# A long convolution with a soft mixture of experts: the order of VectorE's work at the odd part, and the filter's rotation on other engines

## The chip, the cores and the metric

The kernel runs on one core of a Trainium2 chip. The metric is the device time of one execution in microseconds (us); three executions of the kernel before took 959.56, 951.45 and 959.16 us, median 959.16. A core has five engines that run in parallel and wait for each other through semaphores: TensorE (PE in the profile, its weight loads PEld), VectorE (DVE), ScalarE (ACT), GpSimd (POOL), and SyncE (SP), which issues nearly all transfers here. Each engine takes its own instructions strictly in program order, so an instruction that waits holds up everything behind it on its engine. Transfers are done by 16 DMA engines. All data is float32.

## The reference

A causal convolution of 8 sequences of 5696 steps and 128 channels with a filter as long as the sequence, done by FFT, is followed by a mixture of experts with 32 soft slots.

```python
def _attn_ref(x, h):                       # x (8, 5696, 128), h (5696, 128)
    L = 2 * S
    Xf = np.fft.rfft(x, n=L, axis=1)
    Hf = np.fft.rfft(h, n=L, axis=0)
    y = np.fft.irfft(Xf * Hf[None], n=L, axis=1)[:, :S, :]
    return y

def _moe_ref(x, phi, w1, w2):              # x (45568, 128), phi (128, 32)
    logits = x @ phi
    d = softmax of logits over the tokens  # per slot
    slot_input = d.T @ x
    ...                                    # 8 experts on 4 slots each: relu(. @ w1) @ w2
    c = softmax of logits over the slots   # per token
    return c @ slot_out
```

The kernel computes the transform as two stages of matrix products (90 x 64 points). Stage A does the first stage on the inputs, stage B1 the second, the product with the filter's spectrum and stage B2 the first inverse stage; C1 does the last inverse stage, and C2 to C6 are the logits, the two softmaxes and the sums over tokens. Between A and B1, and between B2 and C1, the data goes through DRAM to change its layout (tensors `f` and `z`).

## The kernel before

The front loop goes through steps `t`. "Batch" 0 is the filter `h` itself; batches 1 to 8 are the sequences. In one step run stage A for one chunk of a batch, stage B for one or two units of the batch before it, and one half of the C stages of a pair of chunks of an earlier batch. A batch has 8 steps and 12 units; steps with one and with two units alternate.

Stage A folds the input on GpSimd (even and odd part), multiplies on TensorE, and copies out on ScalarE:

```python
    def fold(c, comp):
        ...
        nc.gpsimd.tensor_tensor(out=y_[:, :, :], in0=t_[:, 0, :, :], in1=t_[:, 1, ::-1, :],
                                op=AL.subtract if comp else AL.add)             # L201

    def stage_a(c, comp):
        ...
        for G in range(2):
            p = bank()
            nc.tensor.matmul(p[:, :], s1[:, tab[G], :], ...)                    # L212
            nc.scalar.activation(st[:, :, G, :], ..., AF.Copy)                  # L214
        # two transfers of st to f
```

Stage B1 is 16 matmuls into the PSUM tile `bt`. For a sequence, VectorE makes four instructions of them. For the filter (`g == 0`), each quarter of the unit is rotated by a phase of its own: ScalarE multiplies by the cosine, VectorE adds the sine's part, and `Hr`, `Hi` are kept for the whole kernel.

```python
    def stage_b1(u):
        ...
        tag = "bz" if g == 0 and w % 2 else "bt"
        bt = bps.tile([P, 2, 2, 2 * D], F32, name="bt", tag=tag)
        ...                                                                     # L250: 16 matmuls
        if g == 0:
            for o, (i, n) in enumerate(us):
                r = slice(0, n * HP)
                for a in range(2):
                    pv = bt[r, a, o, :].rearrange("p (c d) -> p c d", c=2)
                    tag = ("pr", "pi", "yf", "yf")[2 * o + a]
                    pr = bpool.tile([P, 2, D], F32, name="ph", tag=tag, ...)
                    nc.scalar.activation(pr[r, :, :], pv, AF.Copy,
                                         scale=turn[r, 0, i, a:a + 1])          # L261
                    nc.vector.scalar_tensor_tensor(                             # L262
                        out=Hr[r, w, a, o, :], in0=pv[:, 1, :], scalar=turn[r, 1, i, a:a + 1],
                        in1=pr[r, 0, :], op0=AL.mult, op1=AL.add)
                    nc.vector.scalar_tensor_tensor(                             # L265
                        out=Hi[r, w, a, o, :], in0=pv[:, 0, :], scalar=turn[r, 1, i, a:a + 1],
                        in1=pr[r, 1, :], op0=AL.mult, op1=AL.subtract, reverse1=True)
            return
        ...
        for p_, H_ in ((pr, Hr), (pi, Hi)):
            nc.vector.tensor_tensor(out=p_[r, 0:k, :, :], in0=pv, in1=..., op=AL.mult)   # L279
        y_ = bpool.tile([P, 4, 2, D], F32, name="yf", tag="yf", bufs=2)
        for c, op_ in ((0, AL.subtract), (1, AL.add)):
            nc.vector.tensor_tensor(out=y_[r, 0:k, c, :], in0=pr[...], in1=pi[...], op=op_)  # L284
```

Stage B2 (L299) multiplies `yf` into the PSUM tile `bz`, ScalarE copies it out (L304), and it is stored to `z`. A call `slot_b(n)` does B1 of the next unit and B2 of the one before it.

C1 makes an even and an odd part (L354). Its last piece is a function `after`, which the loop calls later. VectorE folds the odd part, and GpSimd makes four sums of it, which C2's transposes (L382) read in the next step:

```python
    def stage_c1(T, between):
        b_, a_ = product(0, 1, 1), product(0, 0, 0)
        nc.scalar.activation(part(0, 0), b_, AF.Copy)
        fold_out(a_, part(0, 0), part(1, 0))        # VectorE, two: L359, L360
        between()                                   # C4
        b_, a_ = product(1, 1, 0), product(1, 2, 1)
        nc.scalar.activation(om[:, :, :], b_, AF.Copy)                          # L367

        def after():
            fold_out(a_, om[:, :, :], op[:, :, :])  # VectorE, two: L359 writes op, L360 writes om
            for v, o_, eng in ((1, op, nc.gpsimd), (0, om, nc.vector if tail else nc.gpsimd)):
                for part_, sign in ((part(v, 1), AL.subtract), (part(v, 0), AL.add)):
                    eng.tensor_tensor(out=part_, in0=part(v, 0), in1=o_[:, :, :], op=sign)   # L373
        ...
        return after
```

The loop's order within a step, the parts that are not touched cut:

```python
    for t in range(last_front + 1):
        if t < NA:
            stage_a(t, 0)
            fold(t + 1, 0)
        if pair(3) is not None:
            dispatch(pair(3))
        if t < last_front:
            slot_b(1)
        ...
        if T is not None:
            after = stage_c1(T, rows)
        ...
        if pair(1) is not None:
            stage_c2(pair(1))
        if pair(5) is not None:
            stage_c6(pair(5))
        slot_b(2)
        ...                       # loads are issued
        if after:
            after()
        if U is not None:
            stage_c5(U)
        if t < NA:
            stage_a(t, 1)
            fold(t + 1, 1)
        if pair(1) is not None:
            stage_c3(pair(1))
        slot_b(3)
        ...                       # column_max, softmax
```

C1 and `after` come in the steps that have one unit, and that unit sits in `slot_b(2)`; the other steps have C2, C3 and two units, in slots 1 and 3.

Of the kernel before, what the change touches and what calls it, by code (L numbers as in the profile page):

```python
# [10 lines left out]
F32 = mybir.dt.float32  # L11
AF = mybir.ActivationFunctionType
AL = mybir.AluOpType
# [9 lines left out]
def transform_tables(S, N1, N2, CH, X0, F0, F1):  # L23

    N, R1, HALF, P = N1 * N2, S // N2, N2 // 2, 2 * N2
    k1 = np.arange(N1)
    alpha = np.pi * (k1 + 0.5) / N1
    m1 = np.arange(R1) - (N1 - 1) / 2
    a1 = np.outer(m1, alpha)  # L40
    s1 = np.stack([np.cos(a1), -np.sin(a1), -np.cos(a1)], 1)
    a0 = np.outer(alpha, np.arange(N1 // 2) + 0.5)
    i1 = np.stack([np.cos(a0), -np.sin(a0), -np.cos(a0)], 1)
    NP = N1 // 2
    part = s1
# [17 lines left out]
    tn = np.zeros((2, N2, 2, NU, 2))  # L63
    for a in range(2):
        wq[a] = w[a * NP:(a + 1) * NP].transpose(1, 0, 2)
        for q in range(NP):
            vq[q % 2, :, q // 2, a] = w[a * NP + q][back].T
            tn[q % 2, :, 0, q // 2, a] = np.cos(turn[a * NP + q]) / N
            tn[q % 2, :, 1, q // 2, a] = np.sin(turn[a * NP + q]) / N
# [5 lines left out]
def kernel(  # L75
# [24 lines left out]
    nc = tc.nc  # L100
    P = 128
    B, S, D = x.shape
# [4 lines left out]
    N1, N2 = 90, 64  # L107
    R1, HALF, NP = S // N2, N2 // 2, N1 // 2
# [7 lines left out]
    HP = P // 2  # L116
# [44 lines left out]
    s1 = apool.tile([P, 3, P], F32, name="s1", tag="s1", bufs=1)  # L161
    wt = fconst.tile([P, NP, HP], F32, name="wt")
    vt = fconst.tile([P, NU, 2, HP], F32, name="vt")
    turn = fconst.tile([P, 2, NU, 2], F32, name="turn")
    Hr = fconst.tile([P, NW, 2, 2, D], F32, name="Hr")
    Hi = fconst.tile([P, NW, 2, 2, D], F32, name="Hi")

# [73 lines left out]
    def stage_b1(u):  # L241
        g, w, us = parts(u)
        t_ = gs.pop(u)
# [4 lines that stand above are left out]
                r = slice(a * HP, (a + 1) * HP)  # L248
                for q in range(n):
                    nc.tensor.matmul(bt[q * HP:(q + 1) * HP, a, o, :], wt[r, 2 * i + q, :],  # L250
                                     t_[r, 2 * o + q, :, :].rearrange("p c d -> p (c d)"),
                                     start=True, stop=True)
        if g == 0:
            for o, (i, n) in enumerate(us):
                r = slice(0, n * HP)
                for a in range(2):
                    pv = bt[r, a, o, :].rearrange("p (c d) -> p c d", c=2)
                    tag = ("pr", "pi", "yf", "yf")[2 * o + a]
                    pr = bpool.tile([P, 2, D], F32, name="ph", tag=tag,
                                    bufs=2 if tag == "yf" else None)  # L260
                    nc.scalar.activation(pr[r, :, :], pv, AF.Copy, scale=turn[r, 0, i, a:a + 1])  # L261
                    nc.vector.scalar_tensor_tensor(  # L262
                        out=Hr[r, w, a, o, :], in0=pv[:, 1, :], scalar=turn[r, 1, i, a:a + 1],
                        in1=pr[r, 0, :], op0=AL.mult, op1=AL.add)
                    nc.vector.scalar_tensor_tensor(  # L265
                        out=Hi[r, w, a, o, :], in0=pv[:, 0, :], scalar=turn[r, 1, i, a:a + 1],
                        in1=pr[r, 1, :], op0=AL.mult, op1=AL.subtract, reverse1=True)
# [8 lines left out]
        pr, pi = [bpool.tile([P, 4, 2, D], F32, name=f"p{c}", tag=f"p{c}") for c in "ri"]  # L276
        for p_, H_ in ((pr, Hr), (pi, Hi)):
            h_ = H_[r, w, :, 0:m, :].rearrange("p a o d -> p (a o) d") if m == 2 else H_[r, w, :, 0, :]
            nc.vector.tensor_tensor(out=p_[r, 0:k, :, :], in0=pv,  # L279
                                    in1=h_.unsqueeze(2).broadcast_to([r.stop, k, 2, D]),  # L280
                                    op=AL.mult)
        y_ = bpool.tile([P, 4, 2, D], F32, name="yf", tag="yf", bufs=2)
        for c, op_ in ((0, AL.subtract), (1, AL.add)):
            nc.vector.tensor_tensor(out=y_[r, 0:k, c, :], in0=pr[r, 0:k, c, :],  # L284
                                    in1=pi[r, 0:k, 1 - c, :], op=op_)
        prods[u] = y_
# [275 lines left out]
    nc.scalar.dma_start(out=turn[:, :, :], in_=t_turn)  # L562
    nc.scalar.dma_start(out=i1[:, :, :], in_=t_i1)
    for comp in range(2):
        fold(0, comp)
# [2 lines left out]
    for t in range(last_front + 1):  # L568
        us = list(units(t))

        def pair(lag):
            T, half = divmod(t - LAG_C - lag, 2)
            return T if half == 0 and 0 <= T < NT else None
# [10 lines left out]
        def slot_b(place=None):  # L584
            if place is not None and place not in turns:
                return
            fresh = bool(us)
            if fresh:
                u = us.pop(0)
                prefetch(u + AHEAD)  # L590
                stage_b1(u)
                wait_b2.append(u)
            if len(wait_b2) > fresh:
                stage_b2(wait_b2.pop(0))
# [276 lines left out]
```

## Time and profile before

| what | value |
|---|---|
| median of three executions | 959.16 us |
| span of the profiled execution | 953.8 us |
| mean granted TensorE clock | 0.94 |
| data moved | 272.44 MB, mean 286 GB/s |
| filter's units in stage B1 | 55 to 119 us |
| C1 in the front loop | from 200 us |
| stage A's last matmul | 705 us |
| front loop's last unit in B1 | 792 us |

How to read the lines: a group or timeline line names the source line, the engine, the operation, and output<-inputs by tile names; x16 is a count; in square brackets stands the idle time of the engine before the instruction and what ended it. A wait line has the total in us, the number of times and the longest. A busy TensorE is not a TensorE at its peak, since the ends of its matmuls are modelled. Four groups that the change touches, from the page (busy us in total, mean ns of one, idle us before and what ended it):

```profile
L201 POOL TENSOR_TENSOR x<-xc 128x512 f32<-128x512 f32 x144 | 196.2, 1370 | 179.7 <-PE bank L212 134.1
...
L284 DVE TENSOR_TENSOR yf<-pr,pi 128x512 f32<-128x512 f32 x192 | 184.8, 1003 | 3.3
L279 DVE TENSOR_TENSOR pr<-bt,Hr 128x1024 f32<-128x1024 f32 x96 | 113.1, 1178 | 88.9 <-PE bt L250 87.3
...
L373 POOL TENSOR_TENSOR y<-y,op 128x512 f32<-128x512 f32 x64 | 77.9, 1217 | 106.6 <-DVE op L359 104.1
```

### The profile page before, as it was taken

To read this page: it belongs to the slowest core of one execution; us is meant where nothing else is said; L and a number is where in the kernel's file an instruction comes from. 1 tells how busy PE (TensorE), PEld (TensorE's weight loads), DVE (VectorE), ACT (ScalarE), POOL (GpSimd) and SP (SyncE) were. 2 spreads that over 40 slices of the span, in tenths; PEclk is the share of its full clock that TensorE was granted. 3 is DMA by queue.
4 is the path that set the end of the run, shared out by engine and by line. 5 is a ranking of instruction groups with operands and counts; after the bars stand their busy time and mean duration, and the time that the engine had idled before them with its cause. 6 is when DMAs were issued, how large, how long until landed. Compare 5 with 4: busy or idle time off the path is not lost.

```text
span 953.8 us, 19381 instructions
## 1 busy us (share of the span) xinstructions
PE 830.5 (87%) x7220; PEld 423.3 (44%) x7220; DVE 688.8 (72%) x972; ACT 501.6 (53%) x934; POOL 429.0 (45%) x385
## 2 busy tenths in 40 slices
PE   6867697879999999999999999999998887777893
PEld 2322243334444444444444444444444443344783
DVE  3024488776987888899889888888888897583552
ACT  3535544444655565656555656555654444375442
POOL 4623333334565555555555555565542334372000
PEclk9979999998999999999999999999999898797865
DMA  9978899999899999998999899999979887862698
GB/s 289 262 236 228 229 308 316 312 332 291 279 284 298 311 296 305 320 311 258 309 304 319 273 319 329 328 288 312 303 255 303 267 292 197 259 226 92 236 405 344
DMA packets 156552, 272.44 MB, mean 286 GB/s; under 512 B 11766, under 2 KB 114422, under 8 KB 153317
## 3 DMA queue, kind: packets, MB, share of 16 engines
q1 hardware_dynamic: 155883, 270.85, 88.7%
q8 instruction: 58, 0.95, 0.4%
q10 hardware_dynamic: 576, 0.36, 0.2%
q14 instruction: 35, 0.29, 0.1%
HBM read 142.85 MB, written 128.21 MB: 284 GB/s over the span
## 4 chain that ended last, share of the span: by engine, by line
PE 42%; DMA 19%; DVE 16%; POOL 13%; issue 5%; ACT 3%; SPq 2%; DVEq 0%; ACTq 0%; POOLq 0%
PE bank L212 14%; PE bank L354 10%; POOL y L373 9%; PE bt L250 7%; DMA gt<-f 5%; DMA out_dram<-o 4%; DVE yf L284 4%; DVE pr L279 4%; DMA f<-fst 4%; DVE pi L279 3%; POOL x L201 3%; PE bz L299 3%; PE bank L391 2%; DMA zd<-z 2%; PE bank L420 2%
## 5 line engine op out<-in xcount | busy, mean ns | idle before, releaser
L212 PE MATMUL bank<-x,s 128*128 128x512 f32 x576 | 281.9, 625 | 23.8 <-POOL x L201 16.9
L201 POOL TENSOR_TENSOR x<-xc 128x512 f32<-128x512 f32 x144 | 196.2, 1370 | 179.7 <-PE bank L212 134.1
L214 ACT ACTIVATE fst<-bank 128x512 f32<-128x512 f32 x288 | 167.1, 597 | 95.0 <-PE bank L212 63.8
L304 ACT ACTIVATE zst<-bz 128x1024 f32<-128x1024 f32 x96 | 93.3, 972 | 183.5 <-PE bz L299 180.5
L284 DVE TENSOR_TENSOR yf<-pr,pi 128x512 f32<-128x512 f32 x192 | 184.8, 1003 | 3.3
L279 DVE TENSOR_TENSOR pr<-bt,Hr 128x1024 f32<-128x1024 f32 x96 | 113.1, 1178 | 88.9 <-PE bt L250 87.3
L212 PEld LDWEIGHTS bank<-x,s 128*128 128x128 f32 x576 | 104.2, 196 | 148.5 <-issue 96.1
L250 PE MATMUL bt<-gt,wt 64*64 64x256 f32 x1620 | 117.8, 397 | 30.9 <-DMA gt<-f 21.5
L373 POOL TENSOR_TENSOR y<-y,op 128x512 f32<-128x512 f32 x64 | 77.9, 1217 | 106.6 <-DVE op L359 104.1
L354 PE MATMUL bank<-zc,i 128*64 128x512 f32 x480 | 116.4, 606 | 2.2 <-DMA zc<-z 1.6
L279 DVE TENSOR_TENSOR pi<-bt,Hi 128x1024 f32<-128x1024 f32 x96 | 112.2, 1169 | 0.0
L299 PE MATMUL bz<-yf,vt 64*64 64x256 f32 x1440 | 102.3, 385 | 5.8 <-DVE yf L284 5.7
L250 PEld LDWEIGHTS bt<-gt,wt 64*64 64x64 f32 x1620 | 54.8, 135 | 109.7 <-issue 38.9
L382 PE MATMUL bank<-ident,y 109*128 109x109 f32 x512 | 66.1, 273 | 19.2 <-POOL y L373 18.4
L262 DVE SCALAR_TENSOR_TENSOR Hr<-bt,turn,ph 128x128 f32<-128x128 f32 (+1 forms) x46 | 16.1, 350 | 81.1 <-ACT ph L261 81.1
L299 PEld LDWEIGHTS bz<-yf,vt 64*64 64x64 f32 x1440 | 58.7, 136 | 31.6 <-issue 10.3
L382 PEld LDWEIGHTS bank<-ident,y 109*128 109x128 f32 x512 | 52.0, 147 | 38.7 <-POOL y L373 29.1
L373 POOL TENSOR_TENSOR y<-y,om 128x512 f32<-128x512 f32 x54 | 64.5, 1195 | 2.1
L384 ACT ACTIVATE yt<-bank 128x360 f32<-128x360 f32 x128 | 54.1, 474 | 15.5 <-PE bank L382 15.2
L354 PEld LDWEIGHTS bank<-zc,i 128*64 128x64 f32 x480 | 29.3, 136 | 63.7 <-issue 44.0
L428 POOL MEMSET dt<- 64x8 f32 x32 | 3.5, 108 | 116.9 <-issue 57.6
L824 PE MATMUL op<-so,cT 32*128 32x128 f32 x704 | 46.2, 368 | 4.3 <-ACT o L833 3.7
(96 smaller groups left out, 876.0 us busy)
## 6 DMA issues: line engine op xcount, KB each, us to landing
f<-fst SPq DMA_DIRECT2D x288, 180.0 KB
gt<-f SPq DMA_DIRECT2D x99, 512.0 KB
z<-zst SPq DMA_DIRECT2D x88, 512.0 KB
zc<-z SPq DMA_DIRECT2D x30, 1024.0 KB
xc<-in_x_dram SPq DMA_DIRECT2D x64, 320.0 KB
out_dram<-o SPq DMA_DIRECT2D x16, 1024.0 KB
zc<-z SPq DMA_DIRECT2D x30, 416.0 KB
out_dram<-o SPq DMA_DIRECT2D x8, 768.0 KB
```

The source lines that it names most:

```text
L201: nc.gpsimd.tensor_tensor(out=y_[:, :, :], in0=t_[:, 0, :, :], in1=t_[:, 1, ::-1, :], op=AL.subtract if comp else AL.add)
L212: nc.tensor.matmul(p[:, :], s1[:, tab[G], :], src[:, :, :].rearrange("p n d -> p (n d)"), start=True, stop=True)
L214: nc.scalar.activation(st[:, :, G, :], p[:, :].rearrange("p (n d) -> p n d", d=D), AF.Copy)
L250: nc.tensor.matmul(bt[q * HP:(q + 1) * HP, a, o, :], wt[r, 2 * i + q, :], t_[r, 2 * o + q, :, :].rearrange("p c d -> p (c d)"), start=True ...
L279: nc.vector.tensor_tensor(out=p_[r, 0:k, :, :], in0=pv, in1=h_.unsqueeze(2).broadcast_to([r.stop, k, 2, D]), op=AL.mult)
L284: nc.vector.tensor_tensor(out=y_[r, 0:k, c, :], in0=pr[r, 0:k, c, :], in1=pi[r, 0:k, 1 - c, :], op=op_)
L299: nc.tensor.matmul(bz[a * HP:(a + 1) * HP, q, o, :], vt[r, i, a, :], y_[r, a * m + o, :, :].rearrange("p c d -> p (c d)"), start=True, sto ...
L304: nc.scalar.activation(st[:, 0:m, 0:n, :].rearrange("p o q x -> p q o x"), bz[:, 0:n, 0:m, :], AF.Copy)
L354: nc.tensor.matmul(p[h_ * HP:(h_ + 1) * HP, :], i1[0:kr, tab, :], t_[0:kr, h_, o, :, q, :], start=True, stop=True)
L373: eng.tensor_tensor(out=part_, in0=part(v, 0), in1=o_[:, :, :], op=sign)
L382: nc.tensor.transpose(p[:, i * TR:(i + 1) * TR], ys[T][0:TR, k * CH + i, 0:D], ident[0:TR, 0:TR])
L384: nc.scalar.activation(yt[:, k * CH:(k + 1) * CH, :, :], of_tokens(p), AF.Copy)
```

## The change

It has two parts. First, `after` is called ahead of `slot_b(2)`, so that VectorE folds the odd part, and GpSimd begins its sums, before VectorE takes up the products and sums of that step's unit. Its instructions are the same; nothing changes on TensorE's own order. Second, the filter's rotation is done like the product of a sequence's unit: VectorE multiplies the whole unit in PSUM by the cosine and by the sine (two instructions of up to 1024 elements a partition), and GpSimd adds and subtracts them into `Hr` and `Hi` (two of up to 512). The four ScalarE copies and eight small VectorE instructions of a unit go. The table `turn` gets a layout that can be read as one operand, and the products use the tiles `pr`, `pi` and, for every second unit, the two `yf` buffers.

```diff
-    turn = fconst.tile([P, 2, NU, 2], F32, name="turn")
+    turn = fconst.tile([P, 2, NW, 2, 2], F32, name="turn")
...
-        if g == 0:
-            for o, (i, n) in enumerate(us):
-                r = slice(0, n * HP)
-                for a in range(2):
-                    pv = bt[r, a, o, :].rearrange("p (c d) -> p c d", c=2)
-                    tag = ("pr", "pi", "yf", "yf")[2 * o + a]
-                    pr = bpool.tile([P, 2, D], F32, name="ph", tag=tag,
-                                    bufs=2 if tag == "yf" else None)
-                    nc.scalar.activation(pr[r, :, :], pv, AF.Copy, scale=turn[r, 0, i, a:a + 1])
-                    nc.vector.scalar_tensor_tensor(
-                        out=Hr[r, w, a, o, :], in0=pv[:, 1, :], scalar=turn[r, 1, i, a:a + 1],
-                        in1=pr[r, 0, :], op0=AL.mult, op1=AL.add)
-                    nc.vector.scalar_tensor_tensor(
-                        out=Hi[r, w, a, o, :], in0=pv[:, 0, :], scalar=turn[r, 1, i, a:a + 1],
-                        in1=pr[r, 1, :], op0=AL.mult, op1=AL.subtract, reverse1=True)
-            return
...
+        tags = ("yf", "yf") if g == 0 and w % 2 else ("pr", "pi")
+        pr, pi = [bpool.tile([P, 4, 2, D], F32, name="p", tag=x, bufs=2 if x == "yf" else 1)
+                  for x in tags]
+        for p_, H_ in ((pr, turn[:, 0]), (pi, turn[:, 1])) if g == 0 else ((pr, Hr), (pi, Hi)):
...                               # h_: the operand, broadcast to the shape of pv
+            nc.vector.tensor_tensor(out=p_[r, 0:k, :, :], in0=pv, in1=h_, op=AL.mult)
+        if g == 0:
+            for c, op_, H_ in ((0, AL.add, Hr), (1, AL.subtract, Hi)):
+                h_ = H_[r, w, :, :, :].rearrange("p a o d -> p (a o) d") if m == 2 else H_[r, w, :, 0, :]
+                nc.gpsimd.tensor_tensor(out=h_, in0=pr[r, 0:k, c, :], in1=pi[r, 0:k, 1 - c, :],
+                                        op=op_)
+            return
...
         if pair(5) is not None:
             stage_c6(pair(5))
+        if after:
+            after()
         slot_b(2)
...
-        if after:
-            after()
         if U is not None:
             stage_c5(U)
```

Cut: the change of the table's layout on the host side, and the load of `turn`, which differs in its shape alone.

More of the change, by code (lines that the diff above doesn't have):

```diff
@@ L62, in transform_tables @@
     vq = np.zeros((2, N2, NU, 2, N2))
-    tn = np.zeros((2, N2, 2, NU, 2))
+    tn = np.zeros((2, N2, 2, (NU + 1) // 2, 2, 2))
     for a in range(2):
@@ L67, in transform_tables @@
             vq[q % 2, :, q // 2, a] = w[a * NP + q][back].T
-            tn[q % 2, :, 0, q // 2, a] = np.cos(turn[a * NP + q]) / N
-            tn[q % 2, :, 1, q // 2, a] = np.sin(turn[a * NP + q]) / N
+            tn[q % 2, :, 0, q // 4, a, q // 2 % 2] = np.cos(turn[a * NP + q]) / N
+            tn[q % 2, :, 1, q // 4, a, q // 2 % 2] = np.sin(turn[a * NP + q]) / N
     wq, vq, tn = [t.reshape(P, *t.shape[2:]) for t in (wq, vq, tn)]
@@ L275, in stage_b1 @@
         k = 2 * m
[L276 to L281, printed above, removed]
+        tags = ("yf", "yf") if g == 0 and w % 2 else ("pr", "pi")
+        pr, pi = [bpool.tile([P, 4, 2, D], F32, name="p", tag=x, bufs=2 if x == "yf" else 1)
+                  for x in tags]
+        for p_, H_ in ((pr, turn[:, 0]), (pi, turn[:, 1])) if g == 0 else ((pr, Hr), (pi, Hi)):
+            if g:
+                h_ = H_[r, w].rearrange("p a o d -> p (a o) d") if m == 2 else H_[r, w, :, 0]
+            else:
+                h_ = (H_[r, w].rearrange("p a o -> p (a o)") if m == 2 else H_[r, w, :, 0]).unsqueeze(2)
+                h_ = h_.broadcast_to([r.stop, k, D])
+            h_ = h_.unsqueeze(2).broadcast_to([r.stop, k, 2, D])
+            nc.vector.tensor_tensor(out=p_[r, 0:k, :, :], in0=pv, in1=h_, op=AL.mult)
[5 more added lines that the diff above has]
+            return
         y_ = bpool.tile([P, 4, 2, D], F32, name="yf", tag="yf", bufs=2)
@@ L561 @@
     nc.scalar.dma_start(out=phi[:, :], in_=moe_phi)
-    nc.scalar.dma_start(out=turn[:, :, :], in_=t_turn)
+    nc.scalar.dma_start(out=turn[:, :, :, :, :], in_=t_turn)
     nc.scalar.dma_start(out=i1[:, :, :], in_=t_i1)
```

## The prediction

> **What bounds the kernel now.** I read the page's busy shares, then a table of stretches, the table of waits, and the timeline of one two-step period.
>
> ```profile
> PE 830.5 (87%) x7220; PEld 423.3 (44%) x7220; DVE 688.8 (72%) x972; ACT 501.6 (53%) x934; POOL 429.0 (45%) x385
> ```
>
> ```profile
> 57.00:119.00 62.00, 45.58 (x240) 18.80 (x244) 28.02 (x92) 36.40 (x78) 20.31 (x16) 0.94 0.78 222
> 228.00:701.00 473.00, 457.51 (x3996) 224.63 (x3994) 406.74 (x527) 278.13 (x504) 267.95 (x230) 1.00 0.95 304
> 701.00:800.00 99.00, 80.44 (x856) 42.43 (x852) 84.06 (x120) 44.37 (x80) 34.79 (x35) 0.91 0.84 263
> ```
>
> The first line is the whole span. The three stretches give length, then busy us of PE, weight load, DVE, ACT and POOL, the clock, the DMA share and GB/s. From 57 to 119 us the filter's units run beside the first batch's forward stage: no engine is busy for more than 74% and the DMA share is only 0.78. From 228 to 701 TensorE is busy 97%, with the DMA engines at 0.95. From 701 on the forward stage has ended and VectorE leads with 85%. Between 119 and 200 us TensorE stops mainly for loads; nothing of the change touches a load.
>
> ```profile
> POOL y L373 <- DVE op L359: 104.1, 29, 7.6
> ...
> DVE Hr L262 <- ACT ph L261: 81.1, 46, 48.0
> ...
> ACT ph L261 <- DVE Hi L265: 24.9, 34, 0.7
> ...
> PE bank L382 <- POOL y L373: 18.4, 38, 1.1
> ...
> PE bank L212 <- POOL x L201: 16.9, 23, 8.7
> ```
>
> Waits over the whole span: total us, times, longest. The second and third are the filter's ping-pong: ScalarE copies a quarter of a unit, VectorE makes two results of it, and ScalarE waits for them before it copies the next. (48 of the 81.1 us is the wait for the first unit.) The other three are one chain: VectorE's fold of the odd part releases GpSimd's four sums, which release the transposes, and behind them GpSimd's fold of the next input releases the forward matmul.
>
> ```profile
> 411.03 1.22 DVE L279 TENSOR_TENSOR pr<-bt,Hr 128x1024 f32<-128x1024 f32 x1
> ...
> 413.42 1.29 DVE L284 TENSOR_TENSOR yf<-pr,pi 128x512 f32<-128x512 f32 x2
> ...
> 414.63 0.68 DVE L359 TENSOR_TENSOR op<-bank,om 128x512 f32<-128x512 f32 x1
> ...
> 415.39 2.44 POOL L373 TENSOR_TENSOR y<-y,op 128x512 f32<-128x512 f32 x2 [3.24 <-DVE op L359]
> ...
> 420.30 0.59 PE L382 MATMUL bank<-ident,y 109*128 109x109 f32 x4 [0.27 <-POOL y L373]
> ...
> 421.52 1.98 PE L212 MATMUL bank<-x,s 128*128 128x512 f32 x4 [0.26 <-POOL x L201]
> ```
>
> The timeline of one period (22.43 us from one moved unit's matmuls to the next): start, length, instruction, idle time before it. The odd part's inputs are ready at 410.1, where the copy to om ends, but VectorE first does a unit's two products and two yf sums, 411.03 to 414.6. So GpSimd idles 3.24 us, finishes its four sums late, and TensorE stops twice.
>
> **What the skill says.** The Trainium skill, "SBUF — State Buffer", section "Who interferes with whom": a VectorE instruction with two SBUF inputs contends with a GpSimd one that reads SBUF, and the second to issue is blocked; with one SBUF input it does not. The trace agrees: the yf sums (two SBUF inputs) take 0.65 us when GpSimd rests and up to 1.77 us, while the products from PSUM stay at 1.22 and the folds of op at 0.68 to 0.69. "GPSIMD Engine Reference", section "2.1 Instruction dispatch": about 2.5 cycles an element for two inputs; at its 1.2 GHz that is an estimate of 1.07 us for 512 elements, and the trace has 1.05 to 1.37. "ScalarE: Activation LUTs", section "What ACT_TABLE_LOAD costs": 186 ns plus 0.833 ns an element plus 93 ns for a pointer operand, an estimate of 492 ns for 256 elements; the trace has 478 for the copies that go.
>
> **The filter, part by part.** Removed: 46 ScalarE copies of 0.478 us (22 us) and 92 small VectorE results of 0.35 us (32 us), which the stretch 57 to 119 consists of. One link takes 1.21 us (copies start at 69.86 and 71.07), so 46 links are 55.7 us of the 62, the rest being the forward stage's own ScalarE copies in between. Added for each of 12 units: two VectorE products of the form that already takes 1.22 us (29 us in all; only 2.4 us of latency a unit) and two GpSimd sums of 512 elements at about 1.2 us (24 x 1.2 = 29 us). GpSimd's 20.3 us in this stretch become 49. TensorE's 45.6 us stay, and moving the same data (62 us x 222 GB/s = 13.8 MB) at the 300 GB/s of the later stages takes 46 us. So three things stand at 46 to 49 us, and GpSimd works in order: the fold of the next input waits behind a sum that waits for products. I take 55 us for the stretch: 7 us gained. It should stay gained, since transfers of the next stage only start earlier.
>
> **The odd part.** Nothing is added; in 27 steps two VectorE folds move ahead of four instructions. In the period shown op would start at 411.03, so GpSimd's sums start when its own row-maximum subtraction ends, at 412.2 instead of 415.4, and end about 417.2. TensorE reaches the transposes at 418.7: both stops vanish. They are 0.53 us of shown idle time; matmul starts, 0.53 us apart at the stop where 0.09 is usual, and as much at the forward matmul, make it about 0.8 us a period. Against it: the products start 1.35 us later, their yf sums at 414.8 fall on GpSimd's busy time and take up to 3 us instead of 1.29, so they end near 418.0, and the matmul of that unit, due at 417.71, waits 0.3. Half a microsecond or so remains: 21 periods x 0.5 = 10. The DMA share of 0.95 would have to become 0.975; I take off a fifth: 8 us. The first period (202 to 228) idles 2.7 us for the same reason, but comes out of the load-bound stage: 1.5. After 701, four periods idle about 2.5 us each for these sums, but there TensorE gets to the moved unit's matmul sooner, and would now wait for yf instead: 2.5 us for all four.
>
> Sum: 7 + 8 + 1.5 + 2.5 = 19; 959 - 19 = 940. The profiled execution took 955.5, so the median lies high in its spread and I put 939.
>
> **Rivals.** (a) GpSimd becomes the filter stage's bound. Its folds sit in one queue with the sums; if each sum waits for its products without overlap, a unit costs 2.4 + 2.4 us in series, the 4.8 of before, and the stage gains nothing and 12 us remain: about 947. For it speaks the in-order queue, against it the two sets of product buffers that alternate. (b) The DMA engines are the true bound from 228 on: the share of 0.95 at 304 GB/s is near the 1.02 at 337 GB/s of the stretch 140 to 160. Then the freed TensorE only waits for loads, or ScalarE for buffers of stores, and the steady stage gives 2 us instead of 8: 946. Against it: TensorE has no wait for a DMA between 228 and 701. (c) VectorE becomes the bound: 20.2 us of a 22.4 us period, plus what the lock adds. If the moved unit's sums cost 2 us more and nothing else gets cheaper, nothing is gained in the steady or the late stage: 951. Against it: the next unit's sums, 2.85 us today because GpSimd works beside them, would fall into a quieter time. (d) Everything goes as meant: the filter stage falls to 50 us, all 0.8 us a period are gained, the late stage gains 2 us a period: 12 + 17 + 2 + 8 = 39, 920.
>
> **Range and chances.** Rivals (a) to (c) would end at 946 to 951, two of them together near 953; (d) at 920. The three times of before spread over 8 us. Range 924 to 954. The 2% line is 940.0, on my estimate: faster by over 2% 0.50, within 2% 0.45. Slower by over 2% needs a blockage that I can't see, such as the filter's sums holding up the forward stage: 0.05.
>
> **What would show it.** The start of the first plain product on bt (119.8 us now) should be near 113. GpSimd's wait for op should fall from 104 us by about 60, the two TensorE waits on GpSimd from 35 us to under 8, and the wait of bz for yf should rise from 5.7 us to some 10. Periods between 228 and 701 should be 0.3 to 0.5 us shorter. The yf sums should show a like total (184.8 us), shifted between units. The prediction is wrong if the first product on bt stays after 117, if TensorE begins to wait for gt or zc between 228 and 701, or if VectorE is busy over 97% there.

## The result and the profile after

| kernel | median us | ratio to the kernel before, with 95% interval |
|---|---|---|
| before, beside it | 956.52 (951.45 to 959.56) | |
| changed | 928.75 (926.44 to 929.01) | 0.9709 [0.9657, 0.9762] |
| changed, measured again | 934.37 (925.43 to 935.86), before 957.83 | 0.9755 [0.9711, 0.9799] |

The change saves 27.8 us (956.52 - 928.75), and 23.5 us in the second measurement. The predicted time was 939, the range 924 to 954.

To see where the time went I cut both traces at the same events: the first plain product on `bt`, the first copy to `om` (the first C1), the second and the 23rd copy to `om`, and the last unit's B1. Each kernel was profiled twice; a cell has the two durations in us, and the last column compares the means.

| stage | before | changed | change of the mean | predicted |
|---|---|---|---|---|
| start to first plain product | 119.8, 118.9 | 108.1, 109.6 | -10.5 | -7 |
| to the first C1 (loads) | 82.3, 80.5 | 79.7, 80.4 | -1.3 | 0 |
| first period with C1 | 26.4, 26.4 | 20.5, 22.1 | -5.1 | -1.5 |
| the next 21 periods | 472.6, 472.5 | 460.6, 463.9 | -10.3 | -8 |
| late stage, to the last unit | 90.6, 90.6 | 90.6, 90.8 | +0.1 | -2.5 |
| the rest (no front loop) | 162.1, 162.9 | 167.1, 167.2 | +4.6 | 0 |

The page's busy line of the changed kernel (busy us, share of the span, instructions):

```profile
PE 820.8 (89%) x7220; PEld 423.8 (46%) x7220; DVE 681.4 (74%) x904; ACT 475.7 (51%) x888; POOL 456.3 (49%) x409
```

The 46 ScalarE copies are gone (934 instructions became 888), and GpSimd has 24 sums more (385 became 409). The table of waits over the whole span (total us, times, longest us):

```profile
DVE p L270 <- PE bt L250: 107.4, 37, 46.0
...
ACT fst L214 <- DMA f<-fst: 59.1, 32, 5.1
...
PE bz L294 <- DVE yf L279: 16.5, 13, 2.3
PE bank L212 <- POOL x L201: 13.0, 8, 8.2
...
POOL y L368 <- DVE op L354: 8.6, 4, 4.1
```

Both parts did their work: the ping-pong's two waits are gone, GpSimd's wait for `op` fell from 104.1 to 8.6 us, and TensorE's wait for the four sums, 18.4 us before, is no longer there. Two waits grew in their place: ScalarE's wait for a free store buffer (`fst`, 23.8 before) and TensorE's for `yf` (5.7 before). The table of stretches (length, busy us of PE, weight load, DVE, ACT, POOL with counts, clock, DMA share, GB/s), of the changed kernel:

```profile
57.00:106.00 49.00, 41.50 (x227) 16.17 (x225) 25.73 (x23) 18.90 (x32) 44.93 (x37) 0.99 0.88 266
187.80:208.40 20.60, 20.40 (x160) 9.21 (x156) 16.71 (x19) 11.88 (x21) 10.59 (x8) 1.00 1.02 332
...
228.00:701.00 473.00, 458.94 (x4135) 229.87 (x4135) 410.07 (x548) 274.48 (x514) 267.50 (x233) 1.00 0.97 310
```

In the filter's stage GpSimd has become the busiest engine (44.93 of 49 us), and the DMA share rose from 0.78 to 0.88. The second line is the first period with C1; it is used below. In the stretch from 228 to 701 us, in whose last 27 us stage A has ended here, the DMA share rose from 0.95 to 0.97. One period of the changed kernel, on its timeline (start, length, instruction, idle before):

```profile
383.68 0.68 DVE L354 TENSOR_TENSOR op<-bank,om 128x512 f32<-128x512 f32 x1
...
384.91 2.45 POOL L368 TENSOR_TENSOR y<-y,op 128x512 f32<-128x512 f32 x2
385.00 1.22 DVE L270 TENSOR_TENSOR p<-bt,Hr 128x1024 f32<-128x1024 f32 x1
...
387.32 2.77 POOL L368 TENSOR_TENSOR y<-y,om 128x512 f32<-128x512 f32 x2
...
387.38 3.26 DVE L279 TENSOR_TENSOR yf<-p 128x512 f32<-128x512 f32 x2
...
391.09 1.04 PE L294 MATMUL bz<-yf,vt 64*64 64x256 f32 x16
...
392.07 1.72 PE L377 MATMUL bank<-ident,y 109*128 109x109 f32 x16
```

GpSimd starts its sums without idling and ends them at 390.1, two microseconds before the transposes at 392.07: TensorE's stop is gone. The price stands in the `yf` line: the two sums took 1.29 us in the period shown of before and take 3.26 here, because they now lie beside GpSimd's four. They end at 390.64, still 0.45 us before the matmul that needs them.

### The profile page after: what moved, and what is told of

Same layout as the page of the kernel before. It is cut to its first block, busy times and chain, and to the rows that moved or that the text cites. A ratio compares the mean times of both kernels' runs of the same rounds, so it can differ in the third digit from the quotient of the medians.

```text
span 926.6 us, 19311 instructions
## 1 busy us (share of the span) xinstructions
PE 820.8 (89%) x7220; PEld 423.8 (46%) x7220; DVE 681.4 (74%) x904; ACT 475.7 (51%) x888; POOL 456.3 (49%) x409
## 4 chain that ended last, share of the span: by engine, by line
PE 52%; DMA 23%; DVE 11%; POOL 4%; SPq 4%; issue 3%; ACT 2%; DVEq 0%; ACTq 0%; POOLq 0%
PE bank L212 17%; DMA f<-fst 10%; PE bank L349 9%; PE bt L250 6%; PE bz L294 6%; PE bank L377 4%; DVE yf L279 4%; DVE p L270 4%; DMA out_dram<-o 4%; DMA zd<-z 3%; PE bank L462 2%; DMA zc<-z 2%; DMA gt<-f 2%; PE bank L415 1%; PE op L819 1%
## 5 line engine op out<-in xcount | busy, mean ns | idle before, releaser
L212 PE MATMUL bank<-x,s 128*128 128x512 f32 x576 | 275.5, 612 | 14.8 <-POOL x L201 13.0
L279 DVE TENSOR_TENSOR yf<-p 128x512 f32<-128x512 f32 x192 | 187.9, 1019 | 3.3
L212 PEld LDWEIGHTS bank<-x,s 128*128 128x128 f32 x576 | 101.8, 192 | 133.6 <-issue 89.0
L270 DVE TENSOR_TENSOR p<-bt,Hr 128x1024 f32<-128x1024 f32 x96 | 112.8, 1175 | 61.9 <-PE bt L250 58.0
L250 PE MATMUL bt<-gt,wt 64*64 64x256 f32 x1620 | 115.5, 392 | 19.1 <-DMA gt<-f 11.9
L294 PE MATMUL bz<-yf,vt 64*64 64x256 f32 x1440 | 102.2, 385 | 16.5 <-DVE yf L279 16.5
L270 DVE TENSOR_TENSOR p<-bt,Hi 128x1024 f32<-128x1024 f32 x96 | 112.2, 1169 | 0.0
L250 PEld LDWEIGHTS bt<-gt,wt 64*64 64x64 f32 x1620 | 54.6, 133 | 95.5 <-issue 22.6
L368 POOL TENSOR_TENSOR y<-y,op 128x512 f32<-128x512 f32 x64 | 77.4, 1210 | 11.2 <-DVE op L354 8.6
L270 DVE TENSOR_TENSOR p<-bt,turn 128x1024 f32<-128x1024 f32 (+1 forms) x24 | 27.2, 1174 | 68.3 <-PE bt L250 49.4
L368 POOL TENSOR_TENSOR y<-y,om 128x512 f32<-128x512 f32 x54 | 72.8, 1348 | 2.1
L377 PE MATMUL bank<-ident,y 109*128 109x109 f32 x512 | 60.7, 277 | 0.7 <-DVE y L368 0.7
L379 ACT ACTIVATE yt<-bank 128x360 f32<-128x360 f32 x128 | 50.9, 480 | 2.8 <-PE bank L377 2.7
```

The costliest lines, as they stand in the source:

```text
L212: nc.tensor.matmul(p[:, :], s1[:, tab[G], :], src[:, :, :].rearrange("p n d -> p (n d)"), start=True, stop=True)
L270: nc.vector.tensor_tensor(out=p_[r, 0:k, :, :], in0=pv, in1=h_, op=AL.mult)
L294: nc.tensor.matmul(bz[a * HP:(a + 1) * HP, q, o, :], vt[r, i, a, :], y_[r, a * m + o, :, :].rearrange("p c d -> p (c d)"), start=True, sto ...
L377: nc.tensor.transpose(p[:, i * TR:(i + 1) * TR], ys[T][0:TR, k * CH + i, 0:D], ident[0:TR, 0:TR])
```

## The experiments

Theory: the two parts act apart from each other; the filter's stage is shorter because the ping-pong is gone, and is now limited by transfers and by GpSimd together; the order frees TensorE in every period, but the transfers take a part of it back; in the late stage the order exchanges one wait for another. The rivals are named with each experiment. Two kernels that leave work out, and the kernel before where it is profiled again, were executed once and have no interval.

### Each part alone

The filter's part alone (in the changed kernel the call is moved back), and the order alone (in the kernel before the call is moved ahead):

```diff
# filter only, on the changed kernel
-        if after:                 # ahead of slot_b(2)
-            after()
...
+        if after:                 # after the loads
+            after()
# order only, on the kernel before: the same move the other way
```

> The filter's rotation as changed, the odd part's sums where they were before. If the two parts act in their own stages: the first plain product on bt near 108 us, the first copy to om near 188 to 190, the periods after it as before (22.4 to 22.8 us), GpSimd's wait for op near 100 us again; time 956.5 - 14 = about 942 us, ratio about 0.985. Rival, the gain of the filter stage is only kept because the later stages are quick enough to use it: the first copy to om back near 200 us, time about 953 us, ratio 0.997.

> The odd part's sums moved, the filter's rotation as before. If the parts act in their own stages: first plain product on bt near 120 us, first copy to om near 202, then a first period about 5 us shorter and 21 periods about 0.57 us shorter, and 0 to 5 us given back behind the front loop; time 956.5 - 14 to - 18 = 939 to 942 us, ratio 0.982 to 0.985, and the two gains add up to the change's 27.8. Rival, the first period's 5.8 us belong to the filter (data had been moved earlier): the first period stays at 26 us here, time about 945 us.

| kernel | median us | ratio, 95% interval | first plain product | first period | 21 periods | late | rest |
|---|---|---|---|---|---|---|---|
| filter only | 946.72 | 0.9913 [0.9887, 0.9939] | 107.3 | 26.6 | 472.4 | 90.6 | 165.5 |
| order only | 941.48 | 0.9861 [0.9800, 0.9922] | 116.6 | 22.7 | 462.9 | 91.6 | 165.8 |

The product of the two ratios is 0.9775, with an interval of some 0.0066 to each side (the root of the two half-widths, 0.0026 and 0.0061, squared and added). That meets both intervals of the changed kernel, so the parts add, as far as these measurements tell. The stages keep them apart too: only the filter's part shortens the first stage by 12 us (the 2 to 3 us of the order alone lie ahead of anything that it moves, and show how far traces differ there), only the order shortens the first period and the 21 that follow, and neither shortens the late stage.

### What limits the filter's stage now

The changed kernel's timeline in this stage, VectorE, GpSimd and TensorE:

```profile
68.55 2.36 DVE L270 TENSOR_TENSOR p<-bt,turn 128x1024 f32<-128x1024 f32 x2 [1.33 <-issue]
68.61 1.27 POOL L274 TENSOR_TENSOR Hi<-p 128x512 f32<-128x512 f32 x1
...
69.84 1.26 POOL L201 TENSOR_TENSOR x<-xc 128x512 f32<-128x512 f32 x1
...
71.16 1.55 PE L212 MATMUL bank<-x,s 128*128 128x512 f32 x3 [0.81 <-POOL x L201]
```

GpSimd works back to back, and TensorE's forward matmul waits 0.81 us for its fold. That reads as if GpSimd were the bound. Two kernels test it: one moves half of the filter's sums to VectorE, the other leaves out all loads of `x` (the filter `h` is still loaded, the sequences are computed from whatever lies in the buffers), which takes 23 of 272 MB away.

```diff
# half of the filter's sums on VectorE
-                nc.gpsimd.tensor_tensor(out=h_, in0=pr[r, 0:k, c, :], ...
+                (nc.vector if c else nc.gpsimd).tensor_tensor(out=h_, in0=pr[r, 0:k, c, :], ...
# no loads of x
-        for r in (slice(0, SPLIT), slice(SPLIT, R1)):
+        for r in (slice(0, SPLIT), slice(SPLIT, R1)) if g == 0 else ():
```

> The changed kernel with one of the filter's two sums on VectorE (0.65 us a unit there when GpSimd rests) instead of GpSimd. Theory, GpSimd is the bound of the filter's stage now (44.9 us busy of the 49 from 57 to 106): the stage loses up to 12 x 1.2 us of GpSimd's time, the first plain product on bt comes near 101 instead of 108 us, where TensorE's 41 us and the transfers stop it, and 3 to 7 us are kept at the end. Rival, the transfers are the bound (share 0.88 at 266 GB/s): the first plain product stays within 2 us of 108.

> The changed kernel without the loads of x (the filter's input h is still loaded; stage A works on what is left in its buffers, so the result is not the convolution). It takes away 23 MB of 272 and nothing else. Theory, the DMA engines are the bound that is left: the filter's stage gets shorter, the first plain product on bt comes near 102 instead of 108 to 110 us, the first copy to om near 175 instead of 188 to 190, the 21 steady periods come down from 461 to 464 to about 454 us, and ScalarE's wait for stores of f falls under 20 us. Rival, GpSimd's queue holds the filter's stage and TensorE the steady one: 107 us, and 460 us.

The stretch of this stage, of the kernel with the divided sums and then of the one without loads of `x` (its stage ends earlier, so its stretch is 44 us):

```profile
57.00:106.00 49.00, 41.00 (x227) 16.34 (x225) 34.09 (x35) 19.11 (x32) 39.28 (x28) 0.99 0.89 272
```

```profile
57.00:101.00 44.00, 36.95 (x218) 14.53 (x218) 23.89 (x21) 16.22 (x28) 40.14 (x33) 1.00 0.78 225
```

With 5.7 us taken off GpSimd (44.93 to 39.28) the first plain product came at 107.3 us; the nine traces that have the filter's part with its sums on GpSimd and all loads lie between 106.7 and 109.6, so this is no difference. The time was 928.46 us, ratio 0.9717 [0.9664, 0.9770], beside 0.9755 [0.9711, 0.9799] of the changed kernel measured with it: no difference that the intervals show. Without the loads of `x` the product came at 103.6 us (908.88 us in all, one execution). But there the filter's first unit began its matmuls at 49.7 us already, in the changed kernel at 53.5 and 54.8. From this start to the first plain product both kernels take 53.9 us, the changed one 54.6 and 54.8: neither edit shortens the stage itself by more than a microsecond. The chain of work that ended last shows what holds it, in the stretches above: the changed kernel, then with the divided sums, then without the loads of `x` (share of the stretch by engine and line; "issue" is time in which the engine waited for nothing that the profile shows):

```profile
by line: PE bank L212 31.3%; DMA xc<-in_x_dram 18.1%; POOL x L201 17.2%; POOL Hi L274 11.8%; issue 9.0%; SPq L218 3.7%; POOL Hr L274 3.1%; SPq L190 2.5%; ACT fst L214 2.5%; SPq L236 1.8%; PE bt L250 1.2%; POOLq L201 0.2%
```

```profile
by line: DMA gt<-f 35.6%; PE bank L212 23.4%; DMA xc<-in_x_dram 9.6%; DMA f<-fst 6.5%; issue 6.3%; POOL x L201 5.2%; PE bt L250 4.5%; SPq L218 3.8%; ACT fst L214 3.7%; SPq L236 1.2%; SPq L190 1.1%; POOL Hr L274 0.1%; POOLq L201 0.1%
```

```profile
by line: POOL x L201 23.3%; POOL Hi L274 22.8%; POOL Hr L274 20.8%; issue 18.7%; PE bank L212 14.3%; PE bt L250 1.3%; POOLq L201 0.0%
```

With GpSimd relieved, its part of the chain falls from 32% to 5% and the transfers' rises from 18% to 52%; without the loads of `x` no transfer is left in it, and GpSimd has 67%. (In the changed kernel's second trace GpSimd has 46% and the transfers 6%.) So the two stand at nearly the same height, and relieving one alone leaves the other. Both at once were not tried. Moving GpSimd's sums elsewhere by itself is not worth it here.

### What the order is worth in the steady stage, and who takes it back

The kernel without loads of `x` tells this too. TensorE's table of waits from 208.4 to 669 us, in the changed kernel:

```profile
PE bank L415 <- ACT fst L214: 5.3, 9, 1.5
PE bank L349 <- DMA zc<-z: 2.2, 3, 1.3
PE bt L250 <- DMA gt<-f: 1.3, 2, 1.0
PE bt L250 <- DVE yf L279: 0.2, 1, 0.2
```

Before, TensorE had no wait for `zc` and none or 0.4 us for `gt` in these periods, but 15.1 and 14.1 us for GpSimd (two traces). Now the waits for GpSimd are gone, and 8.8 of the 9.0 us that remain lead to transfers: to loads, or to ScalarE that could not free a PSUM bank because its store buffer was still being read. The stretch from 228 to 660 us, first the changed kernel and then the one without loads of `x`:

```profile
228.00:660.00 432.00, 422.68 (x3746) 211.33 (x3745) 373.21 (x496) 253.66 (x474) 251.85 (x218) 1.00 0.98 311
```

```profile
228.00:660.00 432.00, 431.23 (x3844) 212.39 (x3836) 387.02 (x503) 262.68 (x479) 254.50 (x220) 1.00 0.88 284
```

In the same 432 us the second did 98 matmuls more, with TensorE busy for all but 0.8 us and the DMA share at 0.88. Its 21 periods took 452.2 us. Measured from 472.5 that is 20.3 us, 0.97 a period; the changed kernel keeps 8.7 to 12.0 of it, and the transfers hold back 8 to 12 us. (The seven other traces with the new order and all work vary more, from 460.2 to 468.0 us; the mean of all nine, 463.8, keeps 8.7 us.) (The kernel before was not run without the loads of `x`; since it had next to no wait for a transfer in these periods, I take it that it would have gained little, and the split of the 20.3 us is an estimate.)

Is it the number of store buffers, or the transfers themselves? A fourth `fst` buffer tells:

```diff
-        st = apool.tile([P, CH, 2, D], F32, name="fst", tag="fst", bufs=3)
+        st = apool.tile([P, CH, 2, D], F32, name="fst", tag="fst", bufs=4)
```

> The changed kernel with four instead of three buffers for stage A's results. Theory, the DMA engines are what is left as the bound in the steady stage: ScalarE's wait for stores of f (59 us) falls, but TensorE then waits longer for loads of gt and zc, and the 21 steady periods stay within 2 us of 460. Rival, it is only the count of buffers: TensorE's 5.4 us of waits behind ScalarE's fst vanish, the steady stage becomes 455, and the time 5 us shorter.

TensorE's waits from 210 to 670 us in this kernel:

```profile
PE bank L349 <- DMA zc<-z: 3.9, 6, 1.3
PE bt L250 <- DMA gt<-f: 2.2, 5, 1.0
...
PE bank L349 <- ACT fst L214: 0.6, 1, 0.6
```

The wait behind `fst` is 0.6 us, where it was 5.3 (6.6 in the changed kernel's second trace). But TensorE's idle time in the 21 periods is 10.1 us, beside 9.3 and 13.0, with 6.1 of it behind `zc` and `gt`, and the periods took 460.2 us, beside 460.6 and 463.9. The buffer was the place where the shortage showed, not its cause. The kernel's time was 925.52 us, 0.9666 [0.9617, 0.9715], better than that of the changed kernel measured with it (0.9755 [0.9711, 0.9799]) with intervals that just touch. In its trace the gain lies in the rest, 160.3 us instead of 167, where no buffer of stage A is in use. What makes it stays open: on top of another edit (below, "the same, four fst") the fourth buffer gave nothing that the intervals show, and the 21 periods took 464.8 us there.

### The late stage: one wait for another

Stage A's last matmuls end 5 us after the 23rd copy to `om`. TensorE's table of waits in this stage, of the kernel before:

```profile
PE bank L382 <- POOL y L373: 8.8, 15, 0.7
PE bank L467 <- ACT d L446: 3.8, 4, 1.0
```

and of the changed kernel:

```profile
PE bz L294 <- DVE yf L279: 9.5, 5, 2.3
PE bank L462 <- ACT d L441: 3.8, 4, 1.0
```

The wait for GpSimd was exchanged for one of the same size for VectorE, and the stage stayed at 90.6 us. The timeline of the changed kernel shows its form:

```profile
688.33 2.45 POOL L368 TENSOR_TENSOR y<-y,op 128x512 f32<-128x512 f32 x2
...
690.73 2.77 POOL L368 TENSOR_TENSOR y<-y,om 128x512 f32<-128x512 f32 x2
690.80 3.25 DVE L279 TENSOR_TENSOR yf<-p 128x512 f32<-128x512 f32 x2
...
694.20 1.09 PE L294 MATMUL bz<-yf,vt 64*64 64x256 f32 x16 [2.03 <-DVE yf L279]
```

The Trainium skill, "SBUF — State Buffer", section "Who interferes with whom", names the cause: these VectorE sums have two SBUF inputs, GpSimd's sums read SBUF, and only one of the two may go at a time. Here VectorE's two sums last as long as GpSimd's last two and a little more. But that GpSimd is the cause, and not the later place in VectorE's own order, has to be shown. Four kernels do that: the old order in the late stage alone; the new order without the two sums that use `om` (left out of the front loop, their `y` halves stay as they were; the `y` buffers are cleared once at the start); and C2 ahead of the other step's first unit, which gives TensorE other work while VectorE is busy. The fourth, twice, keeps all work: in the late stage the `om` sums go to VectorE, behind the `yf` sums.

```diff
# old order while stage A has ended
-        if after:
+        if after and t < NA:
             after()
...
+        if after and t >= NA:     # at the old place
+            after()
# two sums left out
-            for v, o_, eng in ((1, op, nc.gpsimd), (0, om, nc.vector if tail else nc.gpsimd)):
+            for v, o_, eng in ((1, op, nc.gpsimd), (0, om, ...))[:2 if tail else 1]:
# C2 first
+        c2_first = NA <= t < last_front
+        if c2_first and pair(1) is not None:
+            stage_c2(pair(1))     # ahead of slot_b(1), and not at its old place
# om sums on VectorE, late (after gets arguments: which sums, and om's engine)
-            after()
+            after((0, 1) if t < NA else (0,))   # folds and op sums; om sums while t < NA
...
+        if after and t >= NA:     # behind slot_b(2)
+            after((1,), nc.vector)
```

> The changed kernel, but after() moves ahead of the unit only while stage A runs; in the last four or five periods it stands where it was before. Theory: in the late stage the wait of TensorE for GpSimd's sums was only exchanged for one for yf, 0 gained, so this equals the changed kernel within 1.5 us (927 to 930 us), with bz's wait for yf down from 16.5 to about 5 us and the transposes' wait for GpSimd up from 0 to about 9 us. Rival, the late stage does gain the 2.5 us of the prediction and the loss lies in the tail alone: this is 2.5 us slower, 931 us.

> The changed kernel without the two sums of om in the front loop (half of the odd part's four GpSimd sums are left out, and the buffers are cleared once so that they hold numbers). If yf's sums are long because GpSimd's sums of om block them: the pair of yf sums behind op and om falls from 3.26 to about 1.3 us in the late stage and in the steady stage, and bz's wait for yf from 16.5 to under 6 us. Rival, bz waits because VectorE starts the products 1.4 us later: the pair gets shorter, but the wait stays over 10 us.

> The changed kernel with the transposes of stage C2 ahead of slot 1 in the steps without stage A (t from 72 on), so that TensorE does them while VectorE still works at yf. Theory, the late stage gains nothing because the matmul of bz waits for yf ahead of the transposes: that wait falls from 9.5 us to under 3 in the late stage, a late period becomes about 1.4 us shorter, 5 to 7 us in all, ratio about 0.006 lower than the changed kernel's. Rival, VectorE's own chain sets the late period: the wait moves to the transposes or to the products, and under 2 us are gained.

> The changed kernel, but from the end of stage A on the two sums of om run on VectorE behind the unit's yf sums instead of on GpSimd beside them. Theory, the lock between GpSimd's sums and yf costs the late stage its gain: the pair of yf sums after om falls from 3.27 to 1.3 us there, bz's wait for yf from 8.6 to 9.5 us to under 2, the way from the 23rd om to the last unit from 90.7 to about 82 us, and the time is 6 to 9 us under the changed kernel's, ratio about 0.965. Rival, VectorE is the late bound and takes back what the lock gave: under 3 us.

> Both: om's late sums on VectorE and four buffers for stage A's results. If the gains add: ratio 0.955 to 0.962, 914 to 921 us. If four buffers gain nothing of their own and the 0.967 was chance of the run: like the kernel with om's late sums alone.

The late stage in the traces; "at half clock" is the time in it in which the granted TensorE clock was 0.5:

| kernel | late stage us | wait for GpSimd's sums | wait of bz for yf | all idle time of TensorE | at half clock | median us and ratio |
|---|---|---|---|---|---|---|
| before | 90.6 | 8.8 | 0 | 13.1 | 10.6 | |
| changed | 90.6 | 0 | 9.5 | 17.4 | 12.5 | 0.9709 [0.9657, 0.9762] |
| old order late | 89.4 | 7.3 | 0.7 | 12.7 | 14.2 | 933.20, 0.9789 [0.9739, 0.9838] |
| two sums left out | 80.2 | 0 | 0.8 | 11.2 | 0.4 | 921.8, one execution |
| C2 first | 91.7 | 2.4 | 3.5 | 17.4 | 14.3 | 933.51, 0.9748 [0.9700, 0.9795] |
| om sums on VectorE | 86.4 | 0 | 1.5 | 12.6 | 6.9 | 929.41, 0.9675 [0.9629, 0.9721] |
| the same, four fst | 83.2 | 0 | 2.1 | 11.5 | 0 | 925.32, 0.9705 [0.9675, 0.9734] |

A ratio leaves out executions that took over 1.5% longer than the fastest of their kernel: three of six with the `om` sums on VectorE (its trace is of one of these; the median of all six is 0.975 of that of before), one of six with C2 first and with the fourth buffer.

The old order late gained and lost nothing clear: 89.4 us beside 90.6 and 90.8. With two of GpSimd's four sums gone, the two records of a `yf` pair add up to 1.38 us or less throughout this stage, as in an undisturbed pair (five of the changed kernel's thirteen have 3.06 to 3.36), and the wait fell to 0.8 us although VectorE's order was that of the changed kernel. So the lock is the cause, not the order. (In the steady stage the moved pair fell to some 2.4 us only, not to the 1.3 that I expected: there stage A's fold follows on GpSimd and lies beside it.) With the `om` sums on VectorE every pair but the first, whose `om` sums still ran on GpSimd, is short again while all the work is done; that kernel's timeline:

```profile
701.56 1.29 DVE L279 TENSOR_TENSOR yf<-p 128x512 f32<-128x512 f32 x2
702.77 1.42 DVE L370 TENSOR_TENSOR y<-y,om 128x512 f32<-128x512 f32 x2
```

Here the two `om` sums cost VectorE 1.42 us, where GpSimd needed 2.77 beside the lock. The late stage is 4 to 7 us shorter in these two traces, not the 8 to 9 that I expected. Much of that may be the clock: if half of the time at half clock is lost, an estimate, its fall from 12.5 us to 6.9 and 0 is worth 2.8 of the 4.2 us and 6.2 of the 7.4. Whether the shorter waits kept the clock up was not tried. In the time the gain is not resolved: 0.9675 and 0.9705 beside 0.9709 and 0.9755 of the changed kernel, measured apart from them. C2 ahead of the unit failed as its rival said: TensorE reached the transposes earlier and waited for a PSUM bank that VectorE had not read yet (5.8 us) and for GpSimd (2.4).

### The same kernels again

The changed kernel was measured again with the divided sums, the fourth buffer and C2 first, and the kernel before once more, to see whether the longer rest belongs to the change.

> The changed kernel beside the next three on one chip. If its 0.971 is its own: 927 to 931 us, ratio 0.968 to 0.976. If the filter's and the order's gains simply add up as they did one by one (0.9913 x 0.9861 = 0.978): 934 us, ratio 0.976 to 0.980.

> The kernel before a second time, for a second trace of it. From its last unit in stage B1 to the end it took 162.1 us in the first trace, and eight kernels with the change or a part of it took 160 to 167. If that stretch only varies from run to run: 164 to 167 us here as well. Rival, the change lengthens the tail by 3 to 5 us: 161 to 163 us here. The 21 steady periods 472 to 473 us, the first copy to om 200 to 203 us.

The changed kernel's second trace agrees stage by stage with its first within 3.3 us (the table at the top); its ratio does not tell the two expected outcomes apart. The kernel before took 953.65 us, and its rest 162.9, as the rival had it. All twelve traces of kernels with the change or a part of it have a rest of 160.3 to 167.2, mean 164.8, so it is about 2 us longer than before on average, and 4.6 in the two traces of the changed kernel itself. In the changed kernel's rest TensorE ran 85.1 and 88.6 us at half clock, before 76.7 and 81.0. If half of the 8.0 us between the means is lost, an estimate, this makes 4.0 of the 4.6 us. But the kernel with the old order late had 77.0 us at half clock and a rest of 165.8, so the clock alone does not explain it. The instructions there are the same, and the cause stays open.

## Why the prediction was right

The mechanism of both parts was right, and 928.75 lies in the range; the sum of 19 us was 4.5 to 9 us short of the two measured gains, by terms that erred in both directions.

**The filter's stage: 7 predicted, 10.5 measured.** The term for the stretch from 57 us was 55 us where the trace has 51 (57 to 108.1). It held three loads of 46 to 49 us and a loss for GpSimd's order on top. GpSimd's load was sized right (44.9 us busy in the 49 to 106), but the loss did not come: the alternating product buffers kept its sums back to back at 1.26 us. What was left is set by GpSimd and the transfers together, these at 266 GB/s, not at the 300 I used. Rival (a) was half right: GpSimd is one of the two bounds, but the serial chain by which the stage would have gained nothing did not come. That the gain stays was right: the load-bound stage behind it kept its 80 us.

**The first period: 1.5 predicted, 5.1 measured.** I had counted its 2.7 us of idle time and discounted it. Besides, the clock was halved for 6.8 us there, in both traces of before and in the one of the filter's part alone, and in none of the kernels with the new order. The stretch of this period, before and with the filter's part alone; that of the changed kernel is in the result:

```profile
202.10:228.50 26.40, 23.66 (x160) 9.95 (x156) 17.24 (x20) 12.29 (x20) 10.66 (x8) 0.87 1.00 314
```

```profile
186.90:213.50 26.60, 23.69 (x160) 10.15 (x156) 17.21 (x20) 12.30 (x21) 10.66 (x8) 0.87 1.01 320
```

The same 160 matmuls take 23.66 us busy and 20.40 in the changed kernel: 3.3 us, half of the 6.8, beside the 2.5 us of idle time. That the clock is halved at all I did not look for.

**The steady stage: 8 predicted, 10.3 measured (8.7 over all nine traces), by two errors that nearly cancel; that the sum came so close is luck.** The stops were worth more than 0.8 us a period (0.97 without the loads of `x`; 1.7 of the 20.3 us may be 3.4 us at half clock, which both traces of before have in these periods and the changed kernel has not), and the 0.3 us that I took off for the wait of `bz` for `yf` did not come, though the `yf` pair took 3.26 us as foreseen. In the period I read, `op` would have started 6.68 us before that matmul is due; in the one shown after it starts 7.41 before. On the other side the "fifth" for the transfers was too little: they take back about half, 8 to 12 of 20 us. Rival (b) was half right, and the sign that I had named for it, waits for `gt` and `zc` between 228 and 701 us, appeared, 3.5 us of them. The prediction had named it as a sign of being wrong as well, and on what limits this stage it was wrong. The argument against it, that TensorE had no such wait before, was weak: the waits for GpSimd lay over it, and a share of 0.95 left no room.

**The late stage: 2.5 predicted, 0 measured.** I foresaw the wait for `yf` and under-counted it: five waits of up to 2.3 us, 9.5 in all, where I left some 7 for them. Rival (c), VectorE with the lock, holds for this stage alone: there the moved pair lies on the path, and no quieter time follows that would give anything back.

**Signs.** GpSimd's wait for `op` fell by 95 us rather than 60; the engine idles elsewhere instead. TensorE's two waits for GpSimd fell from 35 to 13.0, not under 8: 8.2 of it is the very first fold, which before also had (8.7), and which I had counted as part of the chain. The wait of `bz` for `yf` is 16.5, not 10. The `yf` sums have 187.9 us in all beside 184.8, as predicted. GpSimd paid for the lock too: its `om` sums went from 1195 to 1348 ns each.

## What to carry to other kernels

An early start for a slow engine's work is worth the stop that it removes only where the next resource has room: read the DMA share of that very stage; here, at 0.95, some half of it was kept by the estimate above. A VectorE instruction with two SBUF inputs should not be put beside a run of GpSimd sums when a matmul waits for it soon; find what lies beside it after the move, and check for each stage apart whether the delay reaches the matmul. When an edit removes a wait, the stage stays as long as it was, and a like wait appears elsewhere, as with the fourth buffer, the wait was a symptom.

## What was not expected of the hardware

Short stops of TensorE go with a halved clock. The TensorE timeline of the kernel before, in the first period:

```profile
212.04 0.59 PE L382 MATMUL bank<-ident,y 109*128 109x109 f32 x4 [0.55 <-POOL y L373]
213.71 0.59 PE L382 MATMUL bank<-ident,y 109*128 109x109 f32 x4 [1.08 <-POOL y L373]
215.39 1.22 PE L212 MATMUL bank<-x,s 128*128 128x512 f32 x1 [1.08 <-POOL x L201]
```

The clock record shows 0.5 for 6.8 us from 214.4 on, where the third stop had only begun; two stops, of 0.55 and 1.08 us, lie ahead of it. The last matmul shown takes 1.22 us, about twice the mean of its kind (625 ns). The Trainium skill, "TensorE: Matmul & The Clock Gate", section "Part 1: The HAM clock gate (the "warmup" mystery)", has the clock halved after an idle window of about 3.4 us. The stretches at half clock here, but for the last of each trace, are 3.4 us or a multiple of it, which agrees with such a window, but in this period no single stop was longer than 1.08 us, and matmuls ran between them. The halving comes 12.3 to 12.4 us after the first copy to `om` in all three traces without the new order, and none begins in this period in any trace with it; that the stops cause it is argued from this, not tried by itself.

The other surprise is the size of the lock: a pair of sums went from 1.29 to 3.26 us beside GpSimd's, 2.5 times, while GpSimd's own `om` sums grew by 13% (1195 to 1348 ns). It is mostly VectorE that waits.
